# The first batch of a fused sparse-attention and FFN kernel: strided V issued by ScalarE, casts by pair on three engines, and a fixed order

## The chip, the cores and the metric

One core of a Trainium2 chip. The metric is the device time of one execution in microseconds (us). The names of the profile: PE is TensorE's matmul, PEld its weight load, DVE VectorE, ACT ScalarE, POOL GpSimd, SP SyncE, which issues most DMAs (SPq is its queue).

## The reference

Eight batches of attention with 8 heads, 576 rows and a head size of 64, in fp32; the result goes through a multiplicative feed-forward part.

```python
mask_local = (rel >= 0) & (rel < 32)
mask_strided = (rel >= 0) & (pos[None, :] % 32 == pos[:, None] % 32)
# heads 0 to 3 local, heads 4 to 7 strided; masked scores are -1e9
attn = softmax(scale * q @ k.T); x = attn @ v          # [8*576, 512]
out = ((x @ w1) * (x @ w2)) @ w3 @ w_out               # 512 -> 1024 -> 1024 -> 512
```

## The kernel before

Work is done in fp16 with fp32 sums. Heads are taken by pairs: each batch has pairs 0 and 1 (local) and 2 and 3 (strided). Tokens go through the FFN in nine tiles of 512. w3 and w_out are folded into one matrix (w3 is transposed, L766 and L777, then multiplied, L719, as `w34`).

**Loads.** All loads go through SP, in the order in which the program writes them, into stage tiles `st` in fp32 (nine in rotation), and are cast to fp16 by an engine. For batch 0 that is: q and k of pairs 0 and 1 (rows 0 to 511 of four heads, `load_qk`, L197), the remaining 64 rows of q and k of all heads (`load_rest`), q and k of pairs 2 and 3, local V (four issues, `load_vL`, L197), strided V (two issues, `load_vN`, L238 and L240), then w1 and w2 (L190), w3 (L179) and w_out (L174), then batch 1. Casts of q, k, local V, strided V (L242, L244) and weights are on GpSimd, except k of pairs 0 and 1 (ScalarE) and the remaining rows (VectorE).

**The first batch.** Per pair: transposes of q and k on TensorE (`ah_T1`, L399), copies to `qT` and `kT` (`ah_T1c`: q on ScalarE, k on VectorE; the helper's lines are L88, L90 and L91 for ScalarE, VectorE and GpSimd), transposes of the remaining rows (`ah_R`, L435). The mask is added by TensorE: an identity times a bias tile opens the accumulation in PSUM (`ah_bias`, L492), the scores add to it (`ah_scores`, L480), and exp goes from there to `ptm` or `nptm` (L505). A pair's scores stand in two halves (g = 0, 1), each in a wide bank of the pool `psB` with two buffers. For strided pairs a small copy to `emb` (`ah_tail`, L462) serves the tail rows. `ah_PV` multiplies by V (L537, L541) with a column of ones for the sum; `norm` takes the reciprocal (L551) and multiplies (L552) on VectorE; `ph_T2` transposes back (L560) and copies to `xT` (L88, L571, L573). Then the first FFN tile: products with w1 (`aps`, L667), w2 (`bps`, L676), their product (L679).

**Order.** A scheduler orders each engine's instructions, except those wrapped in `pe()`, which keep the order of the program; before the change these are mainly TensorE's. The order of the first batch on TensorE is the list of `add(...)` calls. In it the scores of both halves of a pair follow the biases of both. `warm` (L820) issues filler matmuls. Before all this stands the set-up on GpSimd, VectorE and TensorE: identity, masks, bias tiles, memsets (L113 to L157, with a small matmul at L121).

After the first batch the rest of the program follows: FFN tiles with the attention of the next batches spread between them, and stores of `out` from SP or ScalarE.

Of the kernel before, what the change touches and what calls it, by code (L numbers as in the profile page):

```python
# [8 lines left out]
FP32 = mybir.dt.float32  # L9
# [10 lines left out]
def kernel(  # L20
# [16 lines left out]
    P = 128  # L37
# [47 lines left out]

    def copy(eng, out, in_):
        if eng == "a":
            return nc.scalar.copy(out=out, in_=in_)  # L88
        elif eng == "v":
            return nc.vector.tensor_copy(out=out, in_=in_)  # L90
        return nc.gpsimd.tensor_copy(out=out, in_=in_)  # L91
# [4 lines left out]
    make_identity(nc, id16)  # L96


# [6 lines left out]
    tmp2 = att.tile([P, 2 * S], FP16, tag="pte", bufs=2, name="tmp2")  # L105
    causal = tmp[:, 0:NW]
    nc.gpsimd.memset(causal, 1.0)
    nc.gpsimd.affine_select(out=causal, in_=causal, compare_op=ALU.is_ge,
                            fill=0.0, base=0, pattern=[[1, NW]], channel_multiplier=-1)
    setup["p"] = nc.gpsimd.affine_select(out=maskE[:, 0:P], in_=causal[:, 0:P], compare_op=ALU.is_ge,  # L110
                                         fill=0.0, base=31, pattern=[[-1, P]], channel_multiplier=1)
    nptms = [ffn.tile([P, 2, 2048], FP16, tag="abt", bufs=4, name="nptm0")]
    nc.gpsimd.memset(emb, 0.0)  # L113

    mps = psF.tile([P, 512], FP32, tag="f")
    sels = []
    for m, lo, n, w in ((8, 208, 18, P), (32, 352, 2, 64), (7, 0, 18, XW), (4, P, 18, YW)):
        sel = tmp[0:m, NW + lo:NW + lo + n * m]
        nc.vector.tensor_copy(out=sel.rearrange("r (t a) -> r t a", a=m),
                              in_=_ap(id16, 0, [[id16.ap[0][0], m], [0, n], [1, m]]))  # L120
        pe(nc.tensor.matmul(mps[0:w, lo:lo + n * m], sel[:, 0:w], sel, start=True, stop=True))  # L121
    for i in range(1, LT):
        lo = 0 if i == 1 else 32
        nc.vector.tensor_copy(out=maskE[:, QL[i] + lo:QL[i + 1] + 32], in_=maskE[:, lo:32 + QL[i + 1] - QL[i]])
    maskN = tmp2[:, 0:NQ]
    nc.vector.memset(maskN[:, NC * NW:NQ], 0.0)
    nc.vector.tensor_mul(maskN[:, 0:NW], mps[:, 208:208 + NW], causal)
    nc.vector.tensor_mul(maskN[0:64, NC * NW:NQ], mps[0:64, 352:416], causal[0:64, 0:64])
    nc.vector.tensor_copy(out=maskN[:, NW:NC * NW].rearrange("p (c x) -> p c x", x=NW),
                          in_=_ap(maskN, 0, [[maskN.ap[0][0], P], [0, NC - 1], [1, NW]]))  # L130
    nc.vector.tensor_copy(out=idw[:, P:2 * P - 32], in_=id16[:, 0:P - 32])
    biasL = tmp[:, S:2 * S]
    for bias, mask in ((biasL, maskL), (biasN, maskN)):
        nc.vector.tensor_scalar(out=bias, in0=mask, scalar1=1.0, scalar2=BIG, op0=ALU.subtract, op1=ALU.mult)
    nc.vector.memset(maskX[:, XC:S], 0.0)
    nc.vector.tensor_mul(maskX[:, 0:XW], mps[0:XW, 0:XW], causal[0:XW, 0:XW])
    nc.vector.tensor_mul(maskX[0:YW, XC:S], mps[0:YW, P:P + YW], causal[0:YW, 0:YW])
    setup["v"] = nc.vector.tensor_copy(out=maskX[:, XW:XC].rearrange("p (c x) -> p c x", x=XW),
                                       in_=_ap(maskX, 0, [[maskX.ap[0][0], XW], [0, XN - 1], [1, XW]]))
# [9 lines left out]
    nc.vector.memset(kT[:, :, S:KW], 0.0)  # L149
    for i in range(2):  # L150
        nc.vector.memset(v16L[i][:, :, :, D], 1.0)
        nc.vector.memset(v16L[i][LQ:P, :, LT - 1, 0:D], 0.0)
        nc.vector.memset(v16X[i][:, :, :, D], 1.0)
        nc.vector.memset(v16X[i][64:P, :, XN, 0:D], 0.0)
    for i in range(2):
        nc.vector.memset(ptms[i][:, S:640], 1.0)
        nc.vector.memset(ptms[i][:, 2 * S:PTW], 1.0)  # L157
# [26 lines left out]
    def load_w12(g):  # L184
        cs = bass.ds(g * 512, 512)
        for wd, wh in ((moe_w1, w1h), (moe_w2, w2h)):
            src = wd.rearrange("(c p) n -> p c n", p=P)
            for c in range(0, KM, 2):
                st = stgp.tile([P, 2, 512], FP32, tag="stg")
                nc.sync.dma_start(st, src[:, c:c + 2, cs])  # L190
                copy("p", wh[:, c:c + 2, cs], st)
# [10 lines left out]
    def load_qk(b, grp, engs="pp"):  # L202
        for nm, ten, eng in (("q", q, engs[0]), ("k", k, engs[1])):
# [4 lines left out]
            with behind(setup["p"] if b == 0 and grp == 0 else None):  # L208
                ins = copy(eng, t, st.rearrange("p h c d -> p c h d"))
            if b == 1:  # L210
                pe(ins)
            x16[(b, nm, grp)] = t

    def load_rest(b, eng="p"):
# [4 lines left out]
        with behind(setup["v"] if b == 0 else None):  # L219
            ins = copy(eng, t, st)  # L220
        if b == 1:
            pe(ins)
        x16[(b, "r")] = t

    def load_vL(b, hps=(0, 1)):
        vt = v16L[b % 2]
        for hp in hps:
# [4 lines left out]
            nc.gpsimd.tensor_copy(out=vt[0:LQ, hs, :, 0:D], in_=st[0:LQ])  # L232
            copy("p", vt[LQ:P, hs, 0:LT - 1, 0:D], vt[0:32, hs, 1:LT, 0:D])

    def load_vN(b):
        vt = v16X[b % 2]
        st = stgp.tile([P, 4, 4 * D], FP32, tag="stg")
        nc.sync.dma_start(st, v[b, 4:8, 0:NM].rearrange("h (p c) d -> p h (c d)", c=4))  # L238
        sy = stgp.tile([64, 4, D], FP32, tag="stg", name="sy")
        nc.sync.dma_start(sy, v[b, 4:8, NM:S].rearrange("h r d -> r h d"))  # L240
        for hs in (slice(0, 2), slice(2, 4)):
            nc.gpsimd.tensor_copy(out=vt[:, hs, 0:NC, 0:D], in_=st[:, hs].rearrange("p h (c d) -> p h c d", c=4))  # L242
            if hs.start == 0:
                nc.gpsimd.tensor_copy(out=vt[0:64, :, NC, 0:D], in_=sy)  # L244
# [148 lines left out]
    def ah_T1(s, i, dst=None):  # L393
        if dst is None:
            dst = psF.tile([P, 2 * NM], FP16, tag="f", name="tps")[:, 0:NM]
        src = x16[(s.b, "qk"[i], s.hp // 2)]
        h0 = 2 * (s.hp % 2)
# [5 lines left out]
    def ah_T1c(s, i, dst):  # L403
        t = (qT, kT)[i]
        eng = "av"[i]
# [53 lines left out]
    def ah_tail(s, g):  # L459
        t, w = ah_home(s)  # L460
        cs, lo, hi = ah_group(s, g)
        return nc.scalar.copy(out=_ap(emb, 640 * (s.hp - 2) + 130 * g, [[emb.ap[0][0], P], [256, 2], [65, 2], [4, 16]]),  # L462
                       in_=_ap(t, ah_off(s, g) + P, [[nptms[s.b].ap[0][0], P], [hi - lo, 2], [NW, 2], [1, 16]]))
# [32 lines left out]
    def ah_S0(s, gs, tails=True):  # L496
# [3 lines left out]
        for g in gs:  # L500
# [3 lines left out]
            if full is not None:  # L504
                nc.scalar.activation(out=o, in_=full[0:kr, :, 0:hi - lo], func=AF.Exp, bias=0.0, scale=scale)  # L505
# [41 lines left out]
    def norm(s, xv, c0, l):  # L547
# [3 lines left out]
        nc.vector.reciprocal(out=rcp[0:w, :, 0:l], in_=xv[:, :, :, D])  # L551
        nc.vector.tensor_mul(s.xqs[0:w, c0:c0 + l].rearrange("p i h d -> p h i d"), xv[:, :, :, 0:D],  # L552
                             _ap(rcp, 0, [[rcp.ap[0][0], w], [LT, 2], [1, l], [0, D]]))

    def ph_T2(s, pool=psM, tag="m"):
# [11 lines left out]
        o = xT[s.hp][:, S * s.b:S * s.b + S]  # L567
        if s.local:
            copy("a", o, ps[:, 0:S])
        elif s.nat:  # L570
            nc.scalar.copy(out=o[:, 0:NM].rearrange("x (p c) -> x p c", c=4),  # L571
                           in_=ps[:, 0:NM].rearrange("x (c p) -> x p c", c=4))
            nc.vector.tensor_copy(out=o[:, NM:S], in_=ps[:, NM:S])  # L573
# [243 lines left out]
    def warm(ps, n):  # L817
        ps = ps.bitcast(FP32)[:, 256:384]
        for _ in range(n):
            pe(nc.tensor.matmul(ps, id16, id16, start=True, stop=True))  # L820

    def ah_Tw(s, i, n):
        ps = psF.tile([P, 2 * NM], FP16, tag="f", name="tps")
        ah_T1(s, i, ps[:, 0:NM])
        warm(ps, n)
        ah_T1c(s, i, ps[:, 0:NM])
# [4 lines left out]

    (a0, b0, c0), (a1, b1, c1), (a2, b2, c2), (a3, b3, c3) = fine
    add(ah_Ti, p0, 0)
    add(both, p0)
    add(ah_Ti, p0, 1)
    add(lambda: rest0.append(ah_R(0)))
    add(ah_S0, p0, (0,))
    add(ah_T, p1)
    add(lambda: rest0[0]())
    add(ah_S0, p0, (1,))  # L840
    add(ah_Tw, p2, 0, 4)
    add(both, p1)
    add(ah_S0, p1, (0, 1))
    add(ah_Ti, p2, 1)
    add(ah_Ti, p3, 0)
    add(ah_Tw, p3, 1, 4)
    add(both, p2)
    add(ah_S0, p2, (0, 1))
    add(ah_PV, p0, 0)
    add(ah_PV, p0, 1)  # L850
    add(both, p3)
    add(ah_S0, p3, (0, 1), False)
    add(ah_PV, p1, 0)
    add(ah_PV, p1, 1)
    add(ph_T2, p0)
    add(lambda: [pe(ah_tail(p3, g)) for g in range(2)])
    add(ah_PV, p2, 0)
    add(ah_PV, p2, 1)
    add(ph_T2, p1)
    add(lambda: a0(0, pool=psB))  # L860
    add(lambda: a1(0, pool=psB))
    add(ah_PV, p3, 0)
    add(ah_PV, p3, 1)
    add(lambda: a2(0, pool=psB))
    add(lambda: a3(0, pool=psB))
    for f in (a0, a1):
        add(f, 1)
    add(ph_T2, p2)
    add(a2, 1)
    add(ph_T2, p3, psF, "f")  # L870
    add(a3, 1)
# [190 lines left out]
```

## Time and profile before

| | |
|---|---|
| three runs | 270.52, 271.12, 271.79 us; median 271.12 |
| profiled execution | 269.93 us, of which the span is 268.2 us |
| granted TensorE clock | 0.997 |
| busy in the span | PE 96%, PEld 51%, DVE 58%, ACT 52%, POOL 37% |
| DMA | 48.69 MB, mean 182 GB/s |

In the profile's rows a group of like instructions is given with start, length, engine, line, operation, output <- input, sizes and count; in square brackets stands the idle time of the engine ahead of it and what ended it. A group's length counts from its first start to its last end, so neighbouring groups overlap by some hundredths.

### The profile page before, as it was taken

The numbers are of one execution on the slowest core, as the hardware profiler recorded it, in microseconds if no ns is written. First come the engines' busy times: TensorE is split into PE (matmuls) and PEld (weight loads), VectorE is DVE, ScalarE is ACT, GpSimd is POOL, SyncE is SP. The second block draws the span as 40 slices with busy tenths as digits, with TensorE's granted clock in tenths as the row PEclk, the third lists the DMA queues.
The fourth block names the chain that finished last, engine by engine and source line by source line (L and its number), as shares of the span: only waits on it lengthen the run. The fifth ranks groups of instructions, "written<-read, shape, count | busy, mean of one in ns | idle before, by whom it ended". The sixth has DMA issues, their size and how long they took to land.

```text
span 268.2 us, 6827 instructions
## 1 busy us (share of the span) xinstructions
PE 257.8 (96%) x2703; PEld 136.4 (51%) x2703; DVE 156.2 (58%) x373; ACT 140.3 (52%) x300; POOL 99.0 (37%) x119
## 2 busy tenths in 40 slices
PE   2999999999999999999999999999999999999993
PEld 1664464565555555555555555555555544444442
DVE  6573533555678766867776777667866752322420
ACT  1774334677566666555556465555466544324331
POOL 5576886778347206511840185038200000000000
PEclk9999999999999999999999999999999999999998
DMA  7999999988597569336923973397330022013013
GB/s 222 260 343 368 409 420 327 257 249 229 174 320 210 181 202 260 116 119 207 291 74 120 268 222 104 123 275 213 100 120 0 2 78 81 0 41 115 2 39 120
DMA packets 61101, 48.69 MB, mean 182 GB/s; under 512 B 31804, under 2 KB 52492, under 8 KB 61068
## 3 DMA queue, kind: packets, MB, share of 16 engines
q1 hardware_dynamic: 57036, 40.97, 50.3%
q10 hardware_dynamic: 4032, 7.28, 7.2%
q8 instruction: 21, 0.34, 0.5%
q14 instruction: 12, 0.10, 0.1%
HBM read 38.80 MB, written 9.44 MB: 180 GB/s over the span
## 4 chain that ended last, share of the span: by engine, by line
PE 85%; DMA 9%; SPq 3%; POOL 1%; issue 0%; ACT 0%; DVE 0%; POOLq 0%
PE ops L719 28%; PE bps L676 21%; PE aps L667 21%; DMA st<-in_moe_w_dram 8%; PE sps L389 3%; SPq L197 3%; PE t2a L586 2%; PE pt L301 2%; PE sps L352 2%; DMA st<-in_v_dram 2%; PE tps L399 1%; PE trp L777 1%; PE sps L480 1%; PE t L560 1%; PE ops L747 0%; PE rps L624 0%
## 5 line engine op out<-in xcount | busy, mean ns | idle before, releaser
L667 PE MATMUL aps<-xT,w1h 128*128 128x512 f16 (+1 forms) x288 | 73.5, 376 | 0.0
L676 PE MATMUL bps<-xT,w2h 128*128 128x512 f16 (+1 forms) x288 | 73.1, 376 | 0.0
L679 DVE TENSOR_TENSOR abt<-bps,asb 128x512 f16<-128x512 f32 (+1 forms) x72 | 48.5, 678 | 36.5 <-PE bps L676 35.0
L91 POOL CAST t<-st 128x1024 f16<-128x1024 f32 (+1 forms) x46 | 45.8, 1004 | 63.5 <-DMA st<-in_q_dram 43.3
L88 ACT COPY asb<-aps 128x512 f32<-128x512 f32 (+1 forms) x71 | 41.4, 584 | 51.2 <-PE aps L667 45.8
L719 PE MATMUL ops<-w,abt 128*128 128x512 f16 x280 | 67.1, 379 | 0.0
L676 PEld LDWEIGHTS <-w2h 128*128 128x128 f16 x288 | 27.1, 98 | 30.9 <-issue 0.7
L667 PEld LDWEIGHTS <-w1h 128*128 128x128 f16 x288 | 26.8, 98 | 28.6 <-issue 0.3
L719 PEld LDWEIGHTS <-abt 128*128 128x128 f16 x280 | 25.2, 98 | 26.2
L730 ACT COPY osb<-ops 128x512 f32<-128x512 f32 x35 | 21.0, 600 | 20.3 <-PE ops L719 19.9
L375 ACT ACTIVATE pte<-sps 128x1024 f16<-128x1024 f32 (+1 forms) x24 | 24.4, 1019 | 13.2 <-PE sps L352 12.8
L552 DVE TENSOR_TENSOR xqs<-sps,rcp 128x768 f16<-128x768 f32 (+1 forms) x24 | 21.4, 891 | 0.8
L364 DVE TENSOR_TENSOR ptm<-pte,maskE 128x1152 f16<-128x1152 f16 (+2 forms) x16 | 12.8, 801 | 7.1 <-ACT pte L375 6.7
L719 PE MATMUL ops<-woh,w3T 128*128 128x512 f16 x64 | 15.3, 380 | 0.0
L90 DVE COPY kT<-pt 128x512 f16<-128x512 f16 (+4 forms) x28 | 11.4, 417 | 6.5 <-ACT kT L88 4.8
L88 ACT COPY qT<-pt 128x224 f16<-128x224 f16 (+4 forms) x40 | 14.9, 422 | 0.2 <-PE pt L309 0.2
L364 DVE TENSOR_TENSOR ptm<-pte,maskX 126x1152 f16<-126x1152 f16 x12 | 10.4, 869 | 7.7 <-ACT pte L375 7.7
L232 POOL CAST v16L<-st 96x768 f16<-96x768 f32 x16 | 13.4, 836 | 3.4 <-DMA st<-in_v_dram 1.8
L260 POOL CAST v16X<-st 126x1024 f16<-126x1024 f32 x6 | 6.9, 1151 | 19.7 <-DMA st<-in_v_dram 19.7
L389 PEld LDWEIGHTS <-ptm 128*128 128x128 f16 (+1 forms) x264 | 11.1, 98 | 5.8 <-DVE ptm L364 0.8
L90 DVE COPY xT<-t2a 128x384 f16<-128x384 f16 (+1 forms) x22 | 8.5, 388 | 7.7 <-PE t2a L586 7.3
L91 POOL COPY v16L<-v16L 32x640 f16<-32x640 f16 x16 | 12.3, 768 | 1.0
(124 smaller groups left out, 274.8 us busy)
## 6 DMA issues: line engine op xcount, KB each, us to landing
st<-in_q_dram SPq DMA_DIRECT2D x16, 512.0 KB, 4.4
st<-in_k_dram SPq DMA_DIRECT2D x16, 512.0 KB, 5.5
st<-in_moe_w_dram SPq DMA_DIRECT2D x16, 512.0 KB, 10.0
out_dram<-osb ACTq DMA_DIRECT2D x27, 256.0 KB, 2.0
st<-in_v_dram SPq DMA_DIRECT2D x32, 144.0 KB
st<-in_v_dram SPq DMA_DIRECT2D x24, 112.0 KB, 2.5
st<-in_moe_w_out_dram SPq DMA_DIRECT2D x4, 512.0 KB, 11.0
out_dram<-osb SPq DMA_DIRECT2D x8, 256.0 KB, 3.9
```

What stands on the lines that cost most here:

```text
L88: return nc.scalar.copy(out=out, in_=in_)
L90: return nc.vector.tensor_copy(out=out, in_=in_)
L91: return nc.gpsimd.tensor_copy(out=out, in_=in_)
L364: nc.vector.tensor_mul(o.rearrange("p (a x) -> p a x", x=x), i.rearrange("p (a x) -> p a x", x=x), _ap(s.mask, lo, [[s.mask.ap[0][0], s.kr ...
L375: nc.scalar.activation(out=pv[0:kr, :, lo:hi], in_=src, func=AF.Exp, bias=0.0, scale=scale)
L389: pe(nc.tensor.matmul(s.ps[:, h, c * 65:c * 65 + 65], s.ptm[0:s.kr, c0:c0 + P], s.v[0:s.kr, 2 * (s.hp % 2) + h, c, :], start=True, stop=True))
L552: nc.vector.tensor_mul(s.xqs[0:w, c0:c0 + l].rearrange("p i h d -> p h i d"), xv[:, :, :, 0:D], _ap(rcp, 0, [[rcp.ap[0][0], w], [LT, 2], [ ...
L667: pe(nc.tensor.matmul(st["a"][:, 0:nt], w1h[:, ci, bass.ds(jc * P, P)], xT[ci][:, tok], start=(ci == 0), stop=(ci == KM - 1)))
L676: pe(nc.tensor.matmul(st["b"][:, 0:nt], w2h[:, ci, bass.ds(jc * P, P)], xT[ci][:, tok], start=(ci == 0), stop=(ci == KM - 1)))
L679: nc.vector.tensor_mul(abts[tch][:, jc, skip:], st["b"][:, 0:nt], st["asb"][:, 0:nt])
L719: pe(nc.tensor.matmul(st["ps"], lhs(ci), rhs(ci), start=(ci == 0), stop=(ci == KF - 1)))
L730: nc.scalar.copy(out=osb, in_=ps)
```

## The change

- Strided V of batch 0 is issued by ScalarE, within its own work, behind the copies of q of pairs 0 and 1; its casts go to VectorE, behind the copies of pair 3.
- q and k of batch 0 are cast pair by pair: q on GpSimd and ScalarE (pairs 0, 1) and GpSimd (2, 3); k on VectorE and GpSimd in turn.
- Copies of qT of pairs 2 and 3 go to VectorE.
- Bias and scores go half by half; the scores of pair 3 go into wide banks like the others.
- Set-up: the memsets of the V tiles go to GpSimd, the bias for local heads is made first, the set-up matmuls use another PSUM pool, and 18 filler matmuls are added around the set-up (8 later ones are dropped).
- The first batch and all casts of weights are pinned to the order of the program on every engine. The first two products with w1 stand ahead of the transposes of pair 1 (`ph_T2(p1)`) and the others are spread between the remaining work of pairs 2 and 3.
- As the scheduler now has other times, three stores of the first tile come earlier in SP's order, ahead of loads of V for batch 2. One copy of q of batch 1 on ScalarE moves ahead of two exps.

The core of the diff:

```diff
+    def pin(ins):
+        return pe(ins) if head[0] else ins
...
-        nc.vector.memset(v16L[i][:, :, :, D], 1.0)
+    def v_ones(i):
+        pe(nc.gpsimd.memset(v16L[i][:, :, :, D], 1.0))
+        pe(nc.gpsimd.memset(v16L[i][LQ:P, :, LT - 1, 0:D], 0.0))
+        pe(nc.gpsimd.memset(v16X[i][:, :, :, D], 1.0))
+        pe(nc.gpsimd.memset(v16X[i][64:P, :, XN, 0:D], 0.0))
...
+    def cast_first(nm, hp, eng):
+        h0 = 2 * (hp % 2)
+        st = stage[(nm, hp // 2)]
+        return copy(eng, x16[(nm, hp)], st[:, h0:h0 + 2].rearrange("p h (c d) -> p c h d", c=4))
...
     def load_vN(b):
+        eng = nc.sync if b else nc.scalar
-        nc.sync.dma_start(st, v[b, 4:8, 0:NM]...)
+        pin(eng.dma_start(st, v[b, 4:8, 0:NM]...))
-        nc.sync.dma_start(sy, v[b, 4:8, NM:S]...)
+        pin(eng.dma_start(sy, v[b, 4:8, NM:S]...))
...
     def ah_T1c(s, i, dst):
-        eng = "av"[i]
+        eng = "v" if i or s.nat and s.b == 0 else "a"
...
+    def batch0():
+        head[0] = True
+        cast_first("q", 0, "p")
+        cast_first("q", 1, "a")
+        both(p0)
+        fill(6)
+        t = [T1(p0, 0), T1(p1, 0)]
+        for s in (p0, p1):
+            ah_T1c(s, 0, t[s.hp])
+        load_vN(0)
+        cast_first("k", 0, "v")
+        cast_first("k", 1, "p")
+        copy("v", *stage["r"])
+        v_ones(1)
+        t = [T1(p0, 1)]
+        ah_T1c(p0, 1, t[0])
+        t.append(T1(p1, 1))
+        rest = ah_R(0)
+        sc(p0, 0)
+        ah_T1c(p1, 1, t[1])
+        rest()
+        sc(p0, 1)
+        for g in range(2):
+            ah_bias(p1, g)
+            sc(p1, g)
+        cast_first("q", 2, "p")
+        cast_first("q", 3, "p")
+        cast_first("k", 2, "v")
+        cast_first("k", 3, "p")
+        t = [T1(p2, 0), T1(p3, 0)]
+        ah_T1c(p2, 0, t[0])
+        ah_T1c(p2, 1, T1(p2, 1))
+        ah_bias(p2, 0)
+        sc(p2, 0)
+        ah_T1c(p3, 0, t[1])
+        ah_T1c(p3, 1, T1(p3, 1))
+        ah_bias(p2, 1)
+        sc(p2, 1)
+        stage["l"][0]()
+        stage["x"]("v")
+        ah_PV(p0, 0)
+        ah_PV(p0, 1)
+        for g in range(2):
+            ah_bias(p3, g)
+            sc(p3, g)
+        stage["l"][1]()
+        ah_tail(p2, 0)
+        ah_tail(p2, 1)
+        ah_PV(p1, 0)
+        ah_PV(p1, 1)
+        ph_T2(p0)
+        ah_tail(p3, 0)
+        ah_tail(p3, 1)
+        ah_PV(p2, 0)
+        ah_PV(p2, 1)
+        head[0] = False
+
+    def batch0b():
+        head[0] = True
+        a0(0, pool=psB)
+        a1(0, pool=psB)
+        ph_T2(p1)
+        ah_PV(p3, 0)
+        a2(0, pool=psB)
+        a3(0, pool=psB)
+        ah_PV(p3, 1)
+        a0(1)
+        a1(1)
+        ph_T2(p2)
+        a2(1)
+        a3(1)
+        ph_T2(p3, psF, "f")
+        head[0] = False
...
-    load_qk(0, 0, "pa")
-    load_rest(0, "v")
-    load_qk(0, 1)
+    load_first(0)
+    load_rest(0)
+    load_first(1)
     load_vL(0)
-    load_vN(0)
+    stream[0]()
+    pos[0] = 1
     load_w12(0)
```

`stage["l"]` holds the casts of local V on GpSimd, `stage["x"]` those of strided V, `stage["r"]` that of the remaining rows; `sc(s, g)` is the scores and the exp of one half; `fill(n)` is n filler matmuls.

More of the change, by code (lines that the diff above doesn't have):

```diff
@@ L122 @@
[L122 to L130, printed above, removed]
@@ L148 @@
     ptms = [consts.tile([P, PTW], FP16, name=f"ptm{i}") for i in range(2)]
-    nc.vector.memset(kT[:, :, S:KW], 0.0)
-    for i in range(2):
-        nc.vector.memset(v16L[i][:, :, :, D], 1.0)
[L152 to L157, printed above, removed]
+    causal = tmp[:, 0:NW]
@@ new lines, with warm @@
+    pe(nc.gpsimd.affine_select(out=maskE[:, 0:P], in_=causal[:, 0:P], compare_op=ALU.is_ge,
+                               fill=0.0, base=31, pattern=[[-1, P]], channel_multiplier=1))
+    v_ones(0)
+    pe(nc.gpsimd.memset(emb, 0.0))
+    pe(nc.vector.memset(kT[:, :, S:KW], 0.0))
+    for i in range(2):
+        pe(nc.vector.memset(ptms[i][:, S:640], 1.0))
+        pe(nc.vector.memset(ptms[i][:, 2 * S:PTW], 1.0))
+    def warm(ps, n, at=256):
+        ps = ps.bitcast(FP32)[:, at:at + P]
+        for _ in range(n):
+            pe(nc.tensor.matmul(ps, id16, id16, start=True, stop=True))
@@ new lines, with to_bias @@
+    warm(psF.tile([P, 1024], FP16, tag="f", name="warm"), 8)
+    for i in range(1, LT):
+        lo = 0 if i == 1 else 32
+        pe(nc.vector.tensor_copy(out=maskE[:, QL[i] + lo:QL[i + 1] + 32], in_=maskE[:, lo:32 + QL[i + 1] - QL[i]]))
+    def to_bias(bias, mask):
+        pe(nc.vector.tensor_scalar(out=bias, in0=mask, scalar1=1.0, scalar2=BIG, op0=ALU.subtract, op1=ALU.mult))
+    to_bias(biasL, maskL)
+    pe(nc.vector.memset(maskN[:, NC * NW:NQ], 0.0))
+    pe(nc.vector.tensor_mul(maskN[:, 0:NW], mps[:, 208:208 + NW], causal))
@@ L207, in load_qk @@
             t = qkp.tile([P, 4, 4, D], FP16, tag=f"{nm}{grp}")
-            with behind(setup["p"] if b == 0 and grp == 0 else None):
-                ins = copy(eng, t, st.rearrange("p h c d -> p c h d"))
+            ins = copy(eng, t, st.rearrange("p h c d -> p c h d"))
             if b == 1:
@@ L218, in load_rest @@
         t = qkp.tile([P, H, D], FP16, tag="r")
-        with behind(setup["v"] if b == 0 else None):
+        if b == 0:
+            stage["r"] = (t, st)
+        else:
             ins = copy(eng, t, st)
-        if b == 1:
-            pe(ins)
+            if b == 1:
+                pe(ins)
         x16[(b, "r")] = t
@@ L815, with T1 @@
     rest0 = []
[L817 to L826, printed above, removed]
+    def T1(s, i):
+        return ah_T1(s, i)
     def both(s):
```

169 lines of the change are left out of this document (81 added, 88 removed).

## The prediction

> **What bounds the kernel now.** I read three views in this order: busy time by stage (are there gaps on TensorE, and where), the chain that ended last (what fills the stretch without gaps), and the timeline of the first 21 us (what each engine waits for there). In the first view, after the stretch, come its length and the busy time of TensorE, weight loads, VectorE, ScalarE and GpSimd, then clock, DMA share and GB/s.
>
> ```profile
> 10.58:18.70 8.12, 7.72 (x132) 5.53 (x131) 4.68 (x14) 7.00 (x15) 6.69 (x9) 1.00 0.95 279
> 18.70:262.00 243.30, 243.17 (x2522) 126.46 (x2522) 144.39 (x321) 128.38 (x278) 87.72 (x98) 1.00 0.56 176
> ```
>
> From 18.70 us on TensorE has 0.13 us of gaps in 243.3 us. Its later work is the same in both programs, so the change can gain only what it brings forward in the first batch, before 18.70. The chain shows a second limit, the weights:
>
> ```profile
> 25.06 10.15 DMA st<-in_moe_w_dram
> ...
> 35.26 1.05 POOL t L91
> ...
> 36.36 0.62 PE trp L766 x8
> ```
>
> At 36.36 us TensorE transposes a block of w3 whose cast ended at 36.31: no slack there. Whatever the head gains, it keeps only as far as the weights come earlier too. So the gain is **the smaller of two numbers**: X, by how much the first batch ends earlier, and Y, by how much the weights land earlier.
>
> **The weights (Y).**
>
> ```profile
> 8.46 1.69 SPq L197 DMA_DIRECT2D st<-in_v_dram  x1
> 10.19 0.82 SPq L238 DMA_DIRECT2D st<-in_v_dram  x1
> 11.06 0.60 SPq L240 DMA_DIRECT2D sy<-in_v_dram  x1
> 11.77 5.21 SPq L190 DMA_DIRECT2D st<-in_moe_w_dram  x8
> ```
> ```profile
> 10.50:13.00 2.50, 2.50 (x49) 1.98 (x47) 1.01 (x2) 2.31 (x6) 2.05 (x4) 1.00 0.78 142
> 13.00:17.50 4.50, 4.21 (x68) 2.67 (x65) 2.46 (x8) 3.78 (x9) 3.65 (x6) 1.00 1.01 329
> ```
>
> The two strided V issues (second and third row) leave SP, so the first weight is issued 11.77 - 10.19 = 1.6 us earlier. The bytes stay the same; what can be won is the stretch in which the DMA engines were underfed, 2.5 us at 142 instead of 329 GB/s, or 2.5 x (1 - 142/329) = 1.4 us. Upper end 1.4. Lower end 0, if the V bytes only push K and local V back. I take 1.0, since the next weights also wait for stage buffers and for earlier loads to land. Y then bounds no X below 1.0.
>
> **The head (X).** VectorE, ScalarE and TensorE in the first batch:
>
> ```profile
> 8.19 0.43 DVE L90 CAST t<-st 128x512 f16<-128x512 f32 x1 [0.65 <-DMA st<-in_k_dram]
> 8.59 0.69 DVE L90 COPY kT<-tps 128x512 f16<-128x512 f16 x1
> ...
> 10.68 0.69 DVE L90 COPY kT<-tps 128x512 f16<-128x512 f16 x1 [0.51 <-PE tps L399]
> 12.68 0.42 DVE L90 COPY kT<-tps 128x512 f16<-128x512 f16 x1 [1.30 <-PE tps L399]
> ...
> 14.73 0.38 DVE L551 RECIPROCAL rcp<-xpl 128x6 f32<-128x6 f32 x2 [0.95 <-PE xpl L537]
> 15.02 0.98 DVE L552 TENSOR_TENSOR xqs<-xpl,rcp 128x384 f16<-128x384 f32 x2
> ```
> ```profile
> 9.83 0.70 ACT L505 ACTIVATE ptm<-sps 128x640 f16<-128x640 f32 x1 [0.24 <-PE sps L480]
> 10.43 0.58 ACT L88 COPY qT<-tps 128x512 f16<-128x512 f16 x1
> 10.91 0.60 ACT L505 ACTIVATE ptm<-sps 128x512 f16<-128x512 f32 x1
> ...
> 12.24 1.19 ACT L505 ACTIVATE ptm<-sps 128x640 f16<-128x640 f32 x2 [0.19 <-PE sps L480]
> ...
> 14.21 1.30 ACT L505 ACTIVATE nptm<-sps 128x576 f16<-128x576 f32 x2 [0.30 <-PE sps L480]
> ```
> ```profile
> 8.68 0.61 PE L435 MATMUL rps<-idw,t 128*128 128x128 f16 x4
> ...
> 10.80 0.40 PE L399 MATMUL tps<-idw,t 128*128 128x128 f16 x4
> ...
> 11.26 0.68 PE L492 MATMUL sps<-tmp,idw 128*128 128x320 f16 x4
> 11.87 0.44 PE L480 MATMUL sps<-qT,kT 64*128 64x96 f16 x14
> 12.24 0.84 PE L399 MATMUL tps<-idw,t 128*128 128x128 f16 x12
> ...
> 16.79 0.52 PE L560 MATMUL t<-idw,xqs 128*128 128x128 f16 x6
> ```
> ```profile
> 5.05 1.04 POOL L91 CAST t<-st 128x1024 f16<-128x1024 f32 x1 [1.95 <-DMA st<-in_q_dram]
> ...
> 13.65 0.82 POOL L232 CAST v16L<-st 96x768 f16<-96x768 f32 x1
> 14.54 0.72 POOL L91 COPY v16L<-v16L 32x640 f16<-32x640 f16 x1
> 15.32 1.18 POOL L242 CAST v16X<-st 128x512 f16<-128x512 f32 x2
> 16.44 0.40 POOL L244 CAST v16X<-sy 64x256 f16<-64x256 f32 x1
> ```
>
> *Set-up and casts by pair: 0.* Eight memsets of the V tiles leave VectorE for GpSimd, the dearest like this:
>
> ```profile
> L152 DVE MEMSET v16L<- 32x256 f16 x2 | 0.5, 272 | 0.2
> ```
>
> The casts of Q are halved over GpSimd and ScalarE, those of K over VectorE and GpSimd (0.43 by the 8.19 row). But in VectorE's order the cast of the remaining 64 rows stands before the copy of kT, and waits for its DMA until 8.19. So kT of pair 0 is copied at 8.59 as before, and the first exp stays at 9.83. That wait hides everything before it; were it gone, at most its 0.65 would be won. What a memset costs on GpSimd the trace doesn't show: between 0 and 8 x 0.3 = 2.4 us, half of them before the first Q at 5.05, half between casts; I take 0 on the path, nearest to the idle 1.95 in the 5.05 row.
>
> *V issued by ScalarE: 0.* It costs ScalarE the 0.82 + 0.60 of the SP rows, behind two qT copies, at some 7.4 to 8.8. Queued behind it is the copy of qT for the remaining rows, whose transposes end at 8.68 + 0.61 = 9.3. Cover 0.5 us; an issue as slow as the 1.69 of the local V above would eat it and cost 0.4.
>
> *Fixed order and halves, pairs 0 and 1: 0.9.* The qT copy between the exps of pair 0 is gone, so the second starts at 10.43, not 10.91. kT of pair 1 is copied behind the small copies, near 10.0, not at 10.68. Bias and scores of pair 1 need only the bank that the first exp frees at 10.5: half of 0.68 and of 0.44 make 0.6, with hand-overs 0.8; exp at 11.3, not 12.24.
>
> *Pairs 2 and 3: gives back 0.2.* Their qT copies move to VectorE (0.42 each as for kT at 12.68). Scores of pair 1 end near 11.9; 12 transposes took 0.84; the kT copy 0.42; four scores 0.3. So exp of pair 2 comes at 13.5, not 14.21: 0.7 earlier. The last kT copy ends near 14.1, behind four more transposes.
>
> *V casts on VectorE: gives back 0.4.* On GpSimd they took 1.18 + 0.40 = 1.6; on VectorE I price them 0.43, 0.43 and 0.27, together 1.1 (between 1.1 and 1.6). They now stand ahead of the first normalisation, which starts at 14.1 + 1.1 = 15.2, not at 14.73. The two of pair 0 took 16.00 - 14.73 = 1.3, so they end at 16.5. Before they ended at 16.00, but TensorE came to the transposes of pair 0 only at 16.79, behind the scores of pair 3. Those scores are now 0.7 earlier, and the normalisation sets this point: 16.5 is **0.3 earlier**. What follows is the same TensorE work, nearly without gaps before, so it moves as one piece; normalisations 3 to 8 run back to back on VectorE and keep the 0.3. The first product with w1 waits for no weight while Y is over 0.
>
> *18 early filler matmuls: 0.1.* Four transposes took 0.61 at 8.68 and 0.40 at 10.80, at a granted clock of 1.00. If an earlier start makes the first group fast, 0.2 of the path to the second exp goes; between 0 and 0.2 I take 0.1. The Trainium skill (TensorE: Matmul & The Clock Gate, Part 1) says that the array runs at half rate until it has been busy for about 3.4 us; by that rule the sum would have the full 0.2. The two rows agree in direction; the granted clock doesn't show it.
>
> *Later output stores earlier in SP's order: 0.* Three now stand before loads of V for batch 2 and wait for ScalarE's copies. The load they hold back longest has 12 us to spare between its cast and its first use:
>
> ```profile
> 72.90 1.05 POOL L260 CAST v16X<-st 126x1024 f16<-126x1024 f32 x1 [4.05 <-DMA st<-in_v_dram]
> ```
> ```profile
> 85.15 0.47 PE L389 MATMUL sps<-v16X,ptm 126*128 126x65 f16 x10
> ```
>
> **Sum.** X = 0.9 - 0.2 - 0.4 + 0.1 = 0.4; Y = 1.0; gain 0.4 us. The profiled execution of 269.93 us (268.2 of it the span) becomes 269.5; the median of the runs shown lies 1.2 above it, at 271.12, and becomes **270.7**.
>
> **Rivals.**
>
> *The full gain.* If the normalisation isn't what sets the pace (the remaining rows land sooner, V casts fall into VectorE's waits, the transposes run fast), X reaches the 0.9 of pair 1 and up to the 0.65 of VectorE's wait at 8.19; Y caps it at 1.4: 271.1 - 1.4 = 269.7. For it: ScalarE loses two copies in its busiest stretch, 7.00 of 8.12. Against it: VectorE takes them all, with five casts.
>
> *VectorE blocked by GpSimd: slower.* In the trace one copy within SBUF took four times its price:
>
> ```profile
> L124 DVE COPY maskE<-maskE 128x128 f16<-128x128 f16 x1 | 0.7, 664 | 0.0
> ...
> L124 DVE COPY maskE<-maskE 128x96 f16<-128x96 f16 x3 | 0.4, 174 | 0.0
> ```
> ```profile
> 5.47 1.03 DVE L124 COPY maskE<-maskE 128x128 f16<-128x128 f16 x5
> ```
>
> It began at 5.47 and ended at 6.13, as GpSimd's cast from 5.05 did (6.09). The V casts fall into GpSimd's 0.82 and 0.72 for local V. Waiting out one and a part costs 1.0, three of them 2.3; normalisation starts at 16.2 to 17.5, and the transposes of pair 0 come 0.7 to 2.0 later than 16.79. Middle: 1.2 slower, 272.3. It decides from a first normalisation at 15.5 on. Against it: GpSimd is done with local V near 15, and a cast to rows of 65 elements may not behave like that copy. The Trainium skill (SBUF — State Buffer, Who interferes with whom) has this as a rule: VectorE copies and casts in their two-port mode and GpSimd instructions exclude each other for the whole instruction. The rows agree; by the rule the sum would be this rival's.
>
> *Nothing reaches the end.* If V bytes from the second queue delay K and local V as much as the weights gain, Y is 0 and whatever X is waits at 36.36: 271.1. Against it: the underfed 2.5 us.
>
> **How the numbers follow.** Forecast 0.50; full gain 0.20; blocked VectorE 0.20; nothing 0.10. About 0.5% (1.36 us) is what a measurement of this kernel can tell from no change: the bounds are 269.8 and 272.5. The full gain ends just beyond the first with 0.14 of its 0.20, the forecast with 0.04 of its 0.50: faster 0.18. The blocked case passes the second with 0.10, and 0.06 is left for slow issues on ScalarE on top of the forecast: slower 0.16. Within: 0.66. The range takes in the full gain and the middle of the blocked case, with 0.1 to 0.4 for the spread of the runs: 269.3 to 272.4.
>
> **What would show it.** Right: first exp near 9.8, exp of pair 1 near 11.3, first normalisation near 15.2, transposes of pair 0 near 16.5, first weight cast at or before 16.5, TensorE without gaps from there, the 142 GB/s stretch gone. Wrong: V casts on VectorE far over 0.43, or starting where GpSimd's instructions end; a gap at the w3 transposes; qT's remaining rows late behind ScalarE's issues; gaps on TensorE in batch 1, which would mean that the reordering reaches beyond the head.

## The result and the profile after

The changed kernel takes **269.62 us** (median of 20 runs, 267.96 to 271.28), the kernel before 271.38 (20 runs, 270.33 to 273.72): a ratio of 0.9933, 95% interval 0.9912 to 0.9953, or 1.8 us less. The forecast was 270.7 with 269.3 to 272.4: the time lies within the range, but 1.1 us below the forecast and below 269.8, from which on the prediction calls the kernel faster (chance 0.18). The two profiled executions don't show this difference: that of before (269.93 us) is one of its shortest, that of after (271.26 us, span 269.5, mean granted clock 0.987) one of its longest. So this section reads the stages, and the experiments settle the difference.

Busy time by stage of the changed kernel, in the columns of before (length, busy time of TensorE, weight loads, VectorE, ScalarE, GpSimd, granted clock, DMA share, GB/s):

```profile
10.58:18.70 8.12, 8.08 (x92) 4.76 (x90) 5.14 (x14) 4.06 (x7) 5.60 (x7) 0.63 1.11 352
18.70:262.00 243.30, 242.54 (x2537) 126.42 (x2536) 146.82 (x326) 129.20 (x283) 88.49 (x98) 1.00 0.55 173
```

DMA no longer pauses in the first batch (352 GB/s, where it was 279), and ScalarE is relieved (4.06 us busy, where it was 7.00). But TensorE, busy throughout, issued 92 matmuls where it issued 132: the granted clock is 0.63. In finer steps:

```profile
8.00:10.00 2.00, 1.37 (x22) 0.86 (x23) 1.80 (x5) 0.81 (x2) 1.76 (x6) 0.96 1.10 325
10.00:12.00 2.00, 1.78 (x18) 0.69 (x17) 0.80 (x3) 1.33 (x3) 1.41 (x2) 0.50 1.15 326
...
14.00:16.00 2.00, 1.96 (x18) 0.95 (x17) 1.28 (x5) 0.65 (x1) 1.09 (x3) 0.50 1.05 378
16.00:18.00 2.00, 2.00 (x29) 1.19 (x28) 1.93 (x6) 1.41 (x2) 1.87 (x2) 0.84 1.05 396
```

From 9.83 to 16.66 us, by the trace's clock records, TensorE runs at half its rate; before, it was 1.00 there from 10.40 us on. The first batch, timeline of ScalarE, then VectorE, then GpSimd:

```profile
9.46 1.19 ACT L556 ACTIVATE ptm<-sps 128x640 f16<-128x640 f32 x2 [0.27 <-DVE kT L95]
11.33 0.70 ACT L556 ACTIVATE ptm<-sps 128x640 f16<-128x640 f32 x1 [0.67 <-PE sps L531]
```
```profile
15.41 0.58 DVE L95 CAST v16X<-st 128x512 f16<-128x512 f32 x1
15.91 0.80 DVE L95 CAST v16X<-sy 64x256 f16<-64x256 f32 x1
16.64 0.41 DVE L95 CAST v16X<-st 128x512 f16<-128x512 f32 x1
```
```profile
15.77 0.79 POOL L96 COPY v16L<-v16L 32x640 f16<-32x640 f16 x1
...
27.26 1.04 POOL L96 CAST t<-st 128x1024 f16<-128x1024 f32 x1 [0.17 <-DMA st<-in_moe_w_dram]
...
33.65 1.04 POOL L96 CAST t<-st 128x1024 f16<-128x1024 f32 x1 [0.20 <-DMA st<-in_moe_w_dram]
```

Both exps of pair 0 now follow each other, and the exp of pair 1 comes at 11.33, as forecast. The V casts on VectorE and the normalisations behind them stand in the chain that ended last:

```profile
15.07 0.42 DVE kT L95
15.49 1.55 DVE v16X L95 x3
```

The small V cast (second VectorE row) takes 0.80 us beside GpSimd's copy within SBUF. The cast of w3 that came at 35.26 comes at 33.65.

For what follows, an execution is cut in **three parts**. The head ends where the chain of waits has its first group of 16 `ops` matmuls (row of before: `40.22 3.56 PE ops L719 x16`, of after: `41.46 3.56 PE ops L771 x16`). The body goes from there to SP's issue of the last store of `out`; the tail from that issue to the end of the span. All in us:

| profiled execution of | span | head | body | tail |
|---|---|---|---|---|
| before | 268.21 | 40.22 | 224.23 | 3.76 |
| after | 269.51 | 41.46 | 225.31 | 2.74 |

The tail is shorter by 1.0 us, though nothing in it was changed.

### The profile page after: what moved, and what is told of

Read it like the earlier page. It is cut to its first block, busy times and chain, and to the rows that moved or that the text cites. A ratio compares the mean times of both kernels' runs of the same rounds, so it can differ in the third digit from the quotient of the medians.

```text
span 269.5 us, 6848 instructions
## 1 busy us (share of the span) xinstructions
PE 262.0 (97%) x2713; PEld 138.3 (51%) x2713; DVE 159.5 (59%) x372; ACT 139.3 (52%) x298; POOL 101.7 (38%) x126
## 4 chain that ended last, share of the span: by engine, by line
PE 88%; DVE 5%; ACT 3%; DMA 2%; SPq 1%; issue 0%; ACTq 0%; DVEq 0%
PE ops L771 28%; PE aps L719 22%; PE bps L728 21%; PE sps L437 3%; DMA st<-in_k_dram 2%; DVE ptm L412 2%; PE t2a L638 2%; PE sps L400 2%; PE pt L349 2%; ACT pte L423 2%; PE tps L450 1%; PE sps L531 1%; PE sps L543 1%; PE t L612 1%; DVE abt L731 1%; ACT asb L93 1%
## 5 line engine op out<-in xcount | busy, mean ns | idle before, releaser
L719 PE MATMUL aps<-xT,w1h 128*128 128x512 f16 (+1 forms) x288 | 73.5, 376 | 0.4 <-DVE abt L731 0.2
L771 PE MATMUL ops<-w,abt 128*128 128x512 f16 x280 | 67.1, 379 | 0.0
L719 PEld LDWEIGHTS <-w1h 128*128 128x128 f16 x288 | 26.9, 98 | 28.6 <-issue 0.7
L771 PEld LDWEIGHTS <-abt 128*128 128x128 f16 x280 | 25.2, 98 | 26.1
L412 DVE TENSOR_TENSOR ptm<-pte,maskX 126x1152 f16<-126x1152 f16 x12 | 11.4, 953 | 7.6 <-ACT pte L423 7.6
L771 PE MATMUL ops<-woh,w3T 128*128 128x512 f16 x64 | 15.3, 380 | 0.0
```

What stands on the lines that cost most here:

```text
L412: nc.vector.tensor_mul(o.rearrange("p (a x) -> p a x", x=x), i.rearrange("p (a x) -> p a x", x=x), _ap(s.mask, lo, [[s.mask.ap[0][0], s.kr ...
L719: pe(nc.tensor.matmul(st["a"][:, 0:nt], w1h[:, ci, bass.ds(jc * P, P)], xT[ci][:, tok], start=(ci == 0), stop=(ci == KM - 1)))
L771: pe(nc.tensor.matmul(st["ps"], lhs(ci), rhs(ci), start=(ci == 0), stop=(ci == KF - 1)))
```

## The experiments

Theory 1 is that of the forecast: the first batch ends earlier, by the smaller of head and weights. Theory 2: TensorE's rate in the first batch decides. Theory 3, stated first ahead of e9: part of the gain lies at the end, outside all work. Parts of every profiled execution (RATE: time of the 12 transposes of one group, 0.84 us at full rate, 1.46 at half):

| | ratio to before, 95% | head | body | tail | RATE |
|---|---|---|---|---|---|
| e1 after again | 0.9944 (0.9913 to 0.9975) | 40.72 | 224.75 | 2.76 | 1.46 |
| e2 V from SP | 0.9950 (0.9926 to 0.9974) | 40.89 | 224.82 | 2.77 | 1.46 |
| e3 no fillers | 0.9933 (0.9910 to 0.9957) | 40.74 | 224.53 | 2.75 | 1.46 |
| e4 gaps filled | 0.9923 (0.9899 to 0.9946) | 39.72 | 225.02 | 2.76 | 0.84 |
| e5 before again | 0.9992 (0.9967 to 1.0017) | 40.11 | 225.98 | 3.75 | 0.84 |
| e6 before, filled | 0.9930 (0.9904 to 0.9957) | 39.69 | 224.49 | 3.05 | 0.84 |
| e7 filled, V casts on GpSimd | 0.9947 (0.9925 to 0.9968) | 40.00 | 225.71 | 2.76 | 0.84 |
| e8 filled, V from SP | 0.9992 (0.9961 to 1.0022) | 42.34 | 224.86 | 2.80 | 0.84 |
| e9 before, memsets on GpSimd | 0.9969 (0.9946 to 0.9993) | 40.25 | 224.45 | 2.75 | 0.84 |
| e10 before, padded | 1.0140 (1.0099 to 1.0180) | - | - | 2.75 | 1.21 |
| e11 before, 8 more on VectorE | 0.9968 (0.9947 to 0.9989) | 40.43 | 226.09 | 2.75 | 0.84 |
| e12 after, 5 more on VectorE | 0.9979 (0.9955 to 1.0003) | 41.03 | 224.68 | 3.20 | 1.46 |

**e1, the changed kernel again.**

> The changed kernel once more, beside the other three of this call. Its one profile shows a granted TensorE clock of 0.50 from 9.9 to 16.7 us. Clock theory (the array is fast early, falls back to half rate in the gaps of the first batch, and how long it stays there differs from run to run): mean granted clocks of the runs spread from 0.987 to 1.00, spans below 267.3 us only near 1.00; ratio to before 0.993, 269.6 us. Weights theory (the runs differ by DMA): the clock says nothing of the span.

270.53 us against 272.0. The mean clocks spread from 0.987 to 1.00 and the three spans below 267.3 us are at 1.00, as the clock theory said; but so is one of 269.8. The profiled execution ran at half rate to 15.44 us, yet its mean granted clock is 1.00: its clock records begin with the switch at 15.44, and what lies ahead of the first record counts as full. So the clock row alone doesn't show a slow start; the transposes do.

```profile
11.42 1.46 PE L450 MATMUL tps<-idw,t 128*128 128x128 f16 x12
```

**e2, strided V issued by SP again.**

```diff
-        eng = nc.sync if b else nc.scalar
+        eng = nc.sync
```

> One part undone: strided V of batch 0 is issued by SP again, at its old place, all else as changed. Weights theory (the gain is the smaller of head and weights, and the weights came 1.6 us earlier because SP issues them earlier): weight casts go back by 1.2 to 1.6 us, TensorE gets a gap of about 1 us at the products with w1 or at the transposes of w3, ratio 0.998 to 1.000 (271.0 to 271.4 us). Rival (head and clock alone make the gain): no gap, ratio stays 0.992 to 0.995.

270.58 us, the rival's ratio. The first weight cast came at 17.64 us (e1: 15.98), but nothing of that reaches the time. While TensorE runs at half rate, the issue by ScalarE is worth nothing that can be measured: the weights are not the limit then.

**e3, the 18 early fillers left out.**

```diff
-    warm(psF.tile([P, 1024], FP16, tag="f", name="warm"), 4)
-    warm(psF.tile([P, 1024], FP16, tag="f", name="warm"), 8)
-        fill(6)
```

> One part undone: the 18 early filler matmuls are left out. Prediction's step (fillers are worth 0.1, at most 0.2 us): 0.1 to 0.2 us above the changed kernel, ratio 0.9935 to 0.994. Clock theory, first form (the early fillers make the array fast too soon, so that it falls back in the gaps): no stretch at 0.50, ratio 0.988 to 0.992. Second form (without them the array is slow longer, and that costs): ratio 0.996 or more, early transposes at 0.6 us a group of four.

269.92 us, the ratio of after. The fillers bring nothing that can be measured as they are.

**e4, sixteen more fillers, in the two gaps on TensorE after them.**

```diff
-        t = [T1(p0, 0), T1(p1, 0)]
+        t = [T1(p0, 0)]
+        tw = psF.tile([P, 2 * NM], FP16, tag="f", name="tps")
+        t.append(ah_T1(p1, 0, tw[:, 0:NM]))
+        warm(tw, 10)
...
+        warm(stage["rps"], 6)
```

> The changed kernel with 16 more filler matmuls in TensorE's gaps between 6.5 and 10.2 us (10 behind the first q transposes, 6 behind the scores of pair 0). Clock theory: the array never falls back, granted clock 0.998 or more in all runs, no stretch at 0.50, and the median falls by about 1 us to 268.5 (ratio 0.989). Rival (the half clock is hidden behind VectorE and the weights): clock goes up, the time stays at 0.993, or is 0.2 to 0.4 us worse as fillers stand ahead of transposes.

269.71 us, the lowest ratio of all, though not apart from e1 by the intervals, and 0.989, which theory 2 forecast, lies outside. The profiled execution is at full rate from 5.17 us on, and its V casts meet no copy of GpSimd:

```profile
11.22 0.84 PE L450 MATMUL tps<-idw,t 128*128 128x128 f16 x12
```
```profile
13.60 0.42 DVE L95 CAST v16X<-st 128x512 f16<-128x512 f32 x1
13.93 0.28 DVE L95 CAST v16X<-sy 64x256 f16<-64x256 f32 x1
14.13 0.41 DVE L95 CAST v16X<-st 128x512 f16<-128x512 f32 x1
14.47 0.18 DVE L602 RECIPROCAL rcp<-xpl 128x6 f32<-128x6 f32 x1
```

First normalisation at 14.47 us (after: 16.96), and the head ends 1.0 us sooner than in e1. The V casts don't stand in its chain; the landing of local V (14.53 us) and GpSimd's casts of it do.

**e5, the kernel before again**, for a second profile.

> The kernel before, for a second profile of it. Its first profile took 269.93 us, while its median on this chip was 272.0: that profile shows 12 transposes at 12.24 us in 0.84 us, full rate, and full rate from 10.2 us on. Rate theory: an ordinary execution of it, near 272, shows the same 12 transposes in 1.46 us and full rate only from 13.4 us or later, and the first product with w1 near 20.5 instead of 18.70. Rival (the order and the weights decide, rate is the same in all): the transposes take 0.84 us again, and the missing 2 us stand as gaps further on.

271.32 us. Theory 2's expectation failed: the execution is 1.6 us longer than the first profile of before, but its transposes took 0.84 us and its head is the same. The 1.7 us are in the body, where its gaps between 60 and 150 us are 1.03 us (first profile 0.07), mostly behind VectorE's products (`abt` 0.7 us, `ptm` 0.2 us):

```profile
60.00:100.00 40.00, 39.40 (x493) 21.40 (x490) 28.38 (x67) 24.22 (x57) 16.86 (x20) 1.00 0.65 197
100.00:150.00 50.00, 49.57 (x590) 25.95 (x590) 35.35 (x81) 28.98 (x67) 19.58 (x22) 1.00 0.59 174
```

By the table, bodies vary from 224.2 to 226.1 us in the old order and from 224.5 to 225.7 in the new. One profile can't tell kernels apart that differ by 0.7%, which is the whole gain.

**e6, the kernel before with 28 early fillers.**

```diff
-    mps = psF.tile([P, 512], FP32, tag="f")
+    warm(psF.tile([P, 1024], FP16, tag="f", name="warm"), 16)
+    mps = psM.tile([P, 512], FP32, tag="m", name="mps")
...
+    warm(psF.tile([P, 1024], FP16, tag="f", name="warm"), 12)
```

> The kernel before with 28 filler matmuls (128x128) in the first 6 us: 16 ahead of the mask products, 12 behind them; nothing else is changed. Rate theory: TensorE is at full rate from about 5.5 us, as where the gaps were filled in the changed kernel, the 12 transposes take 0.84 us in most executions, and the time falls by 1.5 to 2.2 us, to a ratio of 0.992 to 0.995, without any of the change's order, V issue or casts. Rival (order and weights): ratio 0.998 to 1.002.

269.91 us, the whole gain without any of the change, and the ratio that theory 2 forecast. But not for its reason: TensorE is at full rate from 10.30 us, not 5.5, hardly earlier than in before (10.40), and earlier transposes still take half-rate time:

```profile
9.09 1.04 PE L406 MATMUL tps<-idw,t 128*128 128x128 f16 x8
```

The head is 0.4 to 0.5 us shorter than in the two profiles of before, for a reason that isn't shown, and the tail 0.7. That turned the view to the tail.

**e7, as e4, V casts on GpSimd.**

```diff
-        stage["x"]("v")
+        stage["x"]("p")
```

> The changed kernel with the gaps filled (16 more fillers), and the three casts of V for the first batch on GpSimd instead of VectorE. With the gaps filled the first normalisation came at 14.47 behind the three casts (1.1 us). If VectorE's casts set the pace as forecast (0.4 us), the ratio is 0.1 to 0.2% lower than with the gaps filled alone, near 0.991. Rival: GpSimd's casts of V, 1.6 us, push its first weight casts from 16.3 to about 18 and the first product with w1 (17.98) waits for them: ratio 0.993 to 0.996.

270.13 us: the rival's number, not apart from e4 by the intervals, and not by the rival's way: the first weight cast came at 16.61, not 18. The first normalisation came at 14.57, no sooner than 14.47: the casts on VectorE, undisturbed, cost nothing. On GpSimd they push its casts of local V back, and the first product with w1 comes at 18.27 instead of 17.98.

**e8, as e4, V issued by SP** (the edit of e2).

> The changed kernel with the gaps filled, and the strided V issued by SP again. If the weights' landing is a limit once the head is fast, the first weight cast comes 1 to 1.6 us later than 16.32 and the ratio is 0.996 to 0.998 against 0.992 with the gaps filled alone. Rival (the V issue is worth nothing also then): ratio 0.991 to 0.994, as with the gaps filled alone.

271.26 us, apart from e4 by the intervals. A wait of GpSimd, one of TensorE, then a stage of the windows:

```profile
17.72 2.21 POOL L96 CAST w1h<-st 128x1024 f16<-128x1024 f32 x2 [2.62 <-DMA st<-in_moe_w_dram]
```
```profile
17.35 0.36 PE L588 MATMUL xpl<-v16L,ptm 128*128 128x65 f16 x6 [1.04 <-DVE xqs L603]
```
```profile
20.00:22.00 2.00, 2.00 (x14) 1.09 (x13) 1.04 (x4) 0.64 (x1) 1.04 (x1) 0.50 1.01 309
```

The first weight cast comes 1.4 us later than e4's (16.32). V lands later too: VectorE's casts wait for it to 15.64, the normalisation comes at 16.52, TensorE stands for 1.04 us behind it and falls back to half rate from 18.58 to 22.00 us. Once the head is fast, the issue by ScalarE is what keeps it so. The wait that stops TensorE is for V; that the later weights cost anything isn't shown.

**e9, the kernel before with the eight V memsets on GpSimd** (in the four lines that set `v16L` and `v16X`, for both buffers, `nc.vector` becomes `nc.gpsimd`).

> The kernel before with one part of the change alone: the eight memsets of the V tiles are issued by GpSimd instead of VectorE. In both profiles of before, the time from SP's last store to the end of the span is 3.75 us, and in all six of the changed kernel and its variants 2.76; an 8 KB fetch of instructions of 0.7 us falls into the last store's 2.6 us in the former (265.21 us) and after the end in the latter (270.8). Theory of the tail: it is VectorE's (or GpSimd's) stream, whose length changes here by 8 as in the change by 5 to 10; the tail becomes 2.76 and the time falls by 1.0 us, ratio 0.995 to 0.997, less up to 0.3 for the memsets in front of GpSimd's first cast. Rivals: the stream is ScalarE's or SP's, or the tail has another cause: tail 3.75, ratio 0.999 to 1.002.

270.5 us against 271.41. The tail is 2.75, as theory 3 said, and the head (40.25) is no shorter than before: a gain from one part of the change that was priced at nothing.

**e10, the kernel before with 8 memsets on VectorE and 8 copies on ScalarE, into a new tile of 32 bytes per partition.**

```diff
-    add(a3, 1)
+    junk = consts.tile([P, 16], FP16)
+    def pad():
+        a3(1)
+        for i in range(8):
+            pe(nc.vector.memset(junk[:, i:i + 1], 0.0))
+            pe(nc.scalar.copy(out=junk[:, 8 + i:9 + i], in_=id16[:, i:i + 1]))
+    add(pad)
```

> The kernel before with 8 memsets of one column on VectorE and 8 copies of one column on ScalarE, near 20 us, behind the first batch's last normalisation; both engines have slack there (7.9 and 6.8 us busy of 17.6), and the rest of the order stays. Nothing of the change is in it; only the length of two instruction streams differs. Theory of the tail: if the stream is one of these two, its fetch comes 8 instructions sooner, ahead of the last store or of its issue, the tail becomes 2.76 us, and the ratio is 0.995 to 0.998. Rival (the gain is the first batch's and the body's, the tail is chance or belongs to another engine): tail 3.75, ratio 0.999 to 1.002.

275.74 us, ratio 1.014 (1.0099 to 1.018), a miss. The tail was short (2.75 us, as in after), but DMA was slower from the start, long before the added memsets run at 24.41 us:

```profile
6.00:10.60 4.60, 3.59 (x28) 2.10 (x29) 3.13 (x15) 2.02 (x4) 0.81 (x2) 1.00 1.15 283
```

Before:

```profile
6.00:10.60 4.60, 4.03 (x34) 2.69 (x36) 3.18 (x15) 2.57 (x5) 1.13 (x2) 1.00 1.11 327
```

The new tile moves every later buffer by 32 bytes; e11 does without it, and without the copies on ScalarE.

**e11, the kernel before with the 8 memsets on VectorE alone, into a buffer that exists** (against e10).

```diff
-    junk = consts.tile([P, 16], FP16)
     def pad():
         a3(1)
+        junk = att.tile([P, 2, LT], FP32, tag="rcp", name="junk")
         for i in range(8):
-            pe(nc.vector.memset(junk[:, i:i + 1], 0.0))
-            pe(nc.scalar.copy(out=junk[:, 8 + i:9 + i], in_=id16[:, i:i + 1]))
+            pe(nc.vector.memset(junk[:, i % 2, i // 2:i // 2 + 1], 0.0))
```

> The kernel before with 8 memsets of one column added on VectorE near 20 us, into a buffer that it already has (no new memory); nothing of the change is in it. So far the fetch of instructions behind the last store's issue stands where VectorE's count of recorded instructions puts it: 451 (before) at +0.75 us, 450 at +1.50, 446 (the change) at +3.9 to 4.2, 443 at +4.56, 459 none. Theory of the tail: with 459 the fetch is done before the last store, the store's landing is 1.0 us sooner (tail 2.76 instead of 3.75 us), and the ratio is 0.995 to 0.997 although VectorE has more to do. Rival (the gain is the first batch's): ratio 0.999 to 1.002.

270.7 us against 271.34, ratio 0.9968: **eight useless instructions make the kernel before faster.** Here is how it comes about: the DMA engines in the 2.7 us behind SP's last issue, in 40 steps of 0.07 us (share in tenths, GB/s, then a queue). The kernel before:

```profile
DMA  5100000179998997879510010010001000000000
GB/s 183 31 0 0 0 0 0 46 273 341 341 463 319 410 364 266 266 228 281 145 23 23 23 23 0 0 23 0 23 23 46 8 15 23 15 0 0 0 0 0
...
q14 instruction: 1, 0.01, 1.7%
```

The same stretch of e11:

```profile
DMA  4100000279999997989610000000000000000000
GB/s 152 31 0 0 0 0 0 91 273 319 387 341 410 410 387 251 281 243 288 175 31 0 0 0 0 0 0 0 0 0 0 0 0 0 0 0 0 0 0 0
```

And of after:

```profile
DMA  5100000278999997989610000000000000000000
GB/s 183 31 0 0 0 0 0 91 273 296 410 341 387 410 387 243 289 250 281 183 46 0 0 0 0 0 0 0 0 0 0 0 0 0 0 0 0 0 0 0
```

In before, one packet of 8 KB from the instruction queue takes 1.7% of 16 engines' 2.7 us, that is 0.7 us of one engine. The fetch's packet lies between 265.20 and 265.93 us; the other packets of the last stores are done at 265.87, that is 1.4 us after the issue. From 265.92 on sixteen data packets of the stores follow one by one to 266.81 (the row of 23s and what follows it). So one engine, which fetched instructions first, worked on its share alone for another 0.9 us; the trace doesn't name the engine. The span ends with the wait for that store. In after and e11 there is no such packet in the stretch. Where it falls goes by VectorE's count of recorded instructions, semaphores included:

| VectorE's instructions | kernels | fetch, us after SP's last issue | tail |
|---|---|---|---|
| 459, 460 | e10, e11 | before it | 2.75 |
| 452 | e12 | 0.35 | 3.20 |
| 451 | before, e5 | 0.75 and 0.74 | 3.75 |
| 450 | e6 | 1.50 | 3.05 |
| 446 | after, e1 to e4, e8 | 3.88 to 4.22 | 2.74 to 2.80 |
| 443 | e7, e9 | 4.56 | 2.76, 2.75 |

ScalarE's and SP's counts differ between e1 and e2, GpSimd's between e7 and e9, and the fetch doesn't follow them. In e2 and e8 another 8 KB packet starts 0.17 us after the issue and ends at about 0.5 us, when the store's packets begin; the tail stays at 2.77 and 2.80. So it isn't any fetch near the store that costs, but one that runs while the store's packets wait.

**e12, the changed kernel with 5 more instructions on VectorE.**

```diff
+        junk = att.tile([P, 2, LT], FP32, tag="rcp", name="junk")
+        for i in range(5):
+            pe(nc.vector.memset(junk[:, i % 2, i // 2:i // 2 + 1], 0.0))
```

> The changed kernel with 5 memsets of one column added on VectorE near 21 us, into a buffer that it already has: VectorE has 451 recorded instructions again, as before the change. Theory of the tail: the fetch falls into the last store again at +0.75 us, the tail is 3.75 us, and of the change's gain of 0.7% only 0.3% is left: ratio 0.996 to 0.998. Rival (the gain is the first batch's and the body's): ratio 0.992 to 0.995, tail 2.76.

270.79 us against 271.34: of 0.67% a 0.21% is left, as forecast, though by the intervals this is apart neither from no gain nor from e1. The tail of 3.75 us didn't come, since the count became 452, one more than meant. Part of the cost lies ahead of the last copy instead, as the chain's end shows (in before `issue` is 0.01 there):

```profile
265.02 0.37 issue
265.39 0.29 DVE olast L95
```

VectorE's records show the same stop of 0.35 us in before, e5 and e12, each time behind the 447th record. In before that record is the last copy itself, and the stop behind it costs nothing; in e12 it is the wait ahead of the copy. The fetch's packet comes some 0.7 us after the stop. That the stop is VectorE's asking for its instructions is a reading of this place, not a record. The copy is 0.36 us late and the tail 0.45 us longer than after's: 0.8 us together.

## Why the time fell within the range though the reasons were wrong

- **"The change can gain only what it brings forward in the first batch"** is the step that failed. It came from TensorE's gaps, and the view of them ends at 262 us. The largest piece of the gain, 1.0 of 1.8 us, lies in the tail: five fewer instructions on VectorE move a fetch of instructions out of the last store. Shown by e9 and e11, whose ratios exclude 1, and by every trace's tail; e12, the other way round, agrees, though its ratio alone wouldn't show it.
- **What is left for the change itself** is 1.8 - 1.0 = 0.8 us (0.3 to 1.4 by the interval), or by e12, whose penalty is 0.2 us less than that of before, 0.6 - 0.2 = 0.4 (-0.3 to 1.0). The forecast was 0.4. But no profile shows that gain: at half rate, heads of the changed kernel end 0.5 to 1.35 us later than those of before (40.72 to 41.46 against 40.11 and 40.22), at full rate 0.1 to 0.5 us earlier (e7, e4). Bodies vary by more than that. Where the rest of the gain comes from stays open.
- **Fillers, forecast 0.1 (0 to 0.2).** As they are, they are worth nothing that can be measured (e3). The term took TensorE's rate for a small matter, but 12 transposes alone cost 0.62 us more at half rate. By the clock's records TensorE is at full rate from 10.40 us in before; in after it is so from 6.42 to 9.83 and then at half rate to 16.66; in e1 it is at half rate to 15.44, without fillers (e3) to 13.43. The Trainium skill (TensorE: Matmul & The Clock Gate, Part 1) has a free-running window of about 3.4 us that must be busy, and an idle one that takes the rate back. The first half agrees: stretches in the clock's records last 3.41, 6.83 and 252.59 us, whole multiples of 3.41. The second doesn't: after fell back with gaps of only 0.2 to 0.8 us and no idle window. e4, e7 and e8, which fill two of these gaps, stay at full rate through the 12 transposes (0.84 us, where e1 has 1.46). One stretch of 3.41 us at half rate takes a run's mean clock to 0.994, so the runs show how often it happened: 14 of 20 runs of after read 0.994 or less, 6 of 12 of e1, 2 of 12 of e4, none of 6 of e3. The times hardly follow: in after the 14 have a median of 269.64, the other 6 of 269.1.
- **Pairs 0 and 1, forecast 11.3:** 11.33, by luck. From the first exp to that of pair 1 it took 1.87 us instead of 1.5, with biases and scores at half rate, but the first exp came 0.37 us sooner than forecast. **Pairs 2 and 3, forecast 13.5:** 14.53 in after, 13.86 in e1, 12.93 in e4. Of the 1.0 us that after is late, 0.62 are the 12 transposes, priced at 0.84 us, which took 1.46.
- **V casts on VectorE, forecast 1.1 us and a first normalisation at 15.2:** from the first cast to the normalisation it took 0.9 us in e4 (13.60 to 14.47), in after 1.55 us (15.41 to 16.96), 0.5 of it in the small cast beside GpSimd's copy. So the rival "VectorE blocked by GpSimd" did occur, at 0.5 to 0.7 us instead of 1.0 to 2.3. In the chains of after, e1 and e3 the casts stand on the path, as the forecast had it; but TensorE has only 0.04 us of gaps there in after, so how much they cost isn't isolated. In e4's chain they don't stand, and by e7 they give back nothing there.
- **Weights, forecast 1.0:** w3's casts come 1.6 us earlier (35.26 to 33.65), beyond the upper end of 1.4. To a slow head this is worth nothing (e2); in e8, where a fast head loses the issue by ScalarE, it is V's landing that stops TensorE. So "the smaller of two numbers" wasn't put to the test: no experiment shifts the weights alone.
- **V issue on ScalarE at 0** and **set-up at 0:** the issues took 0.48 and 0.70 us at 6.99 and 7.93, and the copy behind them was at 8.93, ahead of the old 9.32: right. The first exp came at 9.46 (8.79 in e1), not 9.83, since the remaining rows landed sooner (their cast starts at 8.01, in e1 at 7.17, where it was 8.19). **Stores at 0:** the V cast for batch 2 went from 72.90 to 76.43, within its 12 us.

That the range holds the time is luck. A gain of 0.4 us was forecast and 1.8 came; the range reached so low only because it took in the rival "the full gain" (269.7), whose conditions didn't come together: the remaining rows landed sooner, but the transposes didn't run fast, and the head is mostly later in the traces. 1.0 us came from a place that the prediction ruled out.

## What to carry to other kernels

Look at what lies behind the last instruction of the chain: the wait for the last store is part of the time, and an instruction fetch that falls into it costs 1 us here, decided by nothing but the length of VectorE's stream. Before a gain under 1% is put down to an edit, lengthen one stream by a few idle instructions and see whether the gain moves. Fillers on TensorE kept its rate up here only where they left few gaps behind them until real work was dense (e4, e7, e8), and even there a gain in time isn't shown.

## What the runs showed of the hardware

- An 8 KB fetch of VectorE's instructions takes 0.3 to 0.7 us in the traces' ends; where it ran ahead of packets of the last store, it cost 1.0 us (before against e11). VectorE stops for 0.35 us, and the packet comes some 0.7 us later (before, e5, e12).
- TensorE fell back to half rate within one execution (0.50 from 9.83 to 16.66 us in after, and from 18.58 to 22.00 us in e8 after a gap of 1.04 us), and the granted clock reads 1.00 in e1 up to 15.44 us while matmuls take the half-rate time.
- A tile of 32 bytes more per partition went with 283 GB/s in place of 327 and 1.4% more time (e10); that the moved addresses are the cause was argued from e11, not tried by itself, and TensorE's rate differs too: it is full only from 14.90 us and at half from 76.34 to 79.75.
- VectorE's bias row of 128x640 took 0.98 us beside a memset on GpSimd (before: 0.31, without one):

```profile
3.84 0.98 DVE L156 TENSOR_SCALAR biasN<-tmp 128x640 f16<-128x640 f16 x1
```
```profile
3.48 1.17 POOL L131 MEMSET emb<- 128x1280 f16 x1
```
